# Attention and experts on one core: modality ids in runs, constants on GpSimd, first k load from ScalarE, another order table

## The chip, the core and the metric

One core of a Trainium2 chip runs the whole kernel. The metric is the time of one execution on the device in microseconds (us). Engines are named as in the profile: PE (TensorE matmul; PEld is its weight load), DVE (VectorE), ACT (ScalarE), POOL (GpSimd), SP (SyncE, which here mostly issues DMAs). An engine works through its own instructions strictly in the order in which they were written, so an instruction that waits holds up all that stand behind it on that engine.

## The reference, cut to what matters

Two stages. First attention with a compressive memory for B=4, H=8, S=576, D=64; its output, as a matrix x of 2304 tokens by 512, then goes through a mixture of 8 experts, of which each token uses one.

```python
scores = scale * q @ k.T                       # causal, 576x576 per head
a = softmax(scores);  local = a @ v
q_p = elu(q) + 1
mem_out = (q_p @ M_prev) / (q_p @ z_prev + 1e-6)
x = g * mem_out + (1 - g) * local              # g = sigmoid(beta), per head

logits = x @ w_gate + modality_bias[modality_id]
e = argmax(logits);  gate_w = softmax(logits)[e]
out = gate_w * (relu(x @ w1[e]) @ w2[e])       # 512 -> 1024 -> 512 per token
```

`modality_id` holds one 64 bit integer (0 or 1) per token. It is needed only as a bias of the gate's logits.

## The kernel before

**Attention** runs over 16 pairs of heads (4 batches of 4 pairs). For each pair: `load_t` fetches q, k and v (two DMAs for q, two for k, three for v, issued by SP into two buffers each, `qn`, `kn`, `vn`); `prep` turns q and k on PE (L617), copies them out of PSUM (`qT`, `kT`, `move`, L605 on ACT or L607 on DVE by the table `ENG`), takes exp(q) on ACT (L630) and makes `ph` from it in three POOL steps (L633, L635, L637); `scores` does q·k on PE (L652), a row minimum with the mask on DVE (L665) and the exp on ACT (L671); `ptrans` turns the probabilities on PE (L688) and copies them to `pt`; `av` multiplies with v (L708); `memory` does the memory read (L739) and `combine` puts both together into `xb` (DVE L777, POOL L782). Once a batch is done, `gate` stores `xb` to `x_dram` (L789), turns it (L801), computes logits (L814) and copies them to `lgs` (L820). `route` makes the expert index of each token and its place in the expert's list, and scatters token numbers into three tables in DRAM, `tbl` (L887); `rank` then counts how many tokens the largest expert has so far (L903, L904).

**Experts.** After the first batch the expert with most tokens is known (`perm0`, L902); `load_w` brings its weights in 16 pieces of 128x512 (L945) through three staging buffers (`xg` twice, `osb`), and splits each into a high part made by ACT (L952) and a low part made by DVE or POOL in turn (L956). `slot` then multiplies 256 gathered tokens: turn (L1009), first matrix (L1031), second (L1053), always as three products of high and low parts. The first slots of the largest expert are mixed into attention's last batches, so that PE has work while it waits there; the rest (another expert's weights, its slots, small remainders) comes when attention is over. A loop at the end does tiles that were left over; here it has none.

**Setup.** `setup` fills constants. POOL writes the mask, zero pads and index rows. DVE makes seven small constants in `small2` (L484 to L490). POOL's `table` (L495) fills a block with a sentinel; it lies in the first part of `xb`, and SP writes it from there into the three tables (L504), plus one zero row (L505). `consts` (L507) loads the gate's weights, the biases and the modality ids: five DMAs put each id into its own partition, 8 bytes each (L513, L515). POOL turns them into a bias per token (`consts2`, L525 to L529).

**The order** of all this is written down by a planner, `Plan`: every step carries an engine, an estimated duration, what it reads and writes, and a priority. The priority is a place in the program plus a number from the table `EARLIER` (stage, part of the program, engine). The planner walks in estimated time and takes for each engine, out of the steps that could start within `WINDOW` of the first one, the one of lowest priority. `ENG` says for each kind of copy, and each quarter of attention, whether ACT or DVE does it. The numbers in both tables were found by a search. While PE has nothing else in the beginning, 90 small matmuls on ones (`warm`, L563) are put into its gaps.

Of the kernel before, what the change touches and what calls it, by code (L numbers as in the profile page):

```python
# [226 lines left out]
def kernel(  # L227
# [89 lines left out]
    EARLIER = {
        "av": ((37990, 64809, -34114, 0, 0), (17172, -53738, 532, 0, 0),
               (-47025, -61069, -2874, 0, 0), (6424, 17552, -8223, 0, 0)),
        "bet": ((0, -613, 17881, 0, -169047), (0, 0, 0, 0, 0), (0, 0, 0, 0, 0), (0, 0, 0, 0, 0)),  # L320
        "c": ((1994, 0, 12754, -23788, 0), (349, 0, 2076, -62209, 0),
              (3614, 0, -9647, -56606, 0), (44924, 0, 7322, -42973, 0)),
        "con": ((0, 0, -18237, -36160, -17681), (0, 0, 0, 0, 0), (0, 0, 0, 0, 0), (0, 0, 0, 0, 0)),
# [1059 lines left out]
```

## Time and profile before

| | |
|---|---|
| median of 3 runs | 457.66 us (457.32 to 458.00) |
| the profiled execution | 458.25 us, of which the profile's span is 456.5 us |
| PE busy | 432.2 us, 95% of the span, 4230 instructions |
| DVE, ACT, POOL busy | 241.5, 234.3, 202.4 us (53, 51, 44%) |
| mean granted clock of PE | 0.976 |
| DMA | 42.96 MB, 82092 packets, 70848 of them under 512 B |

The shares are means over two very different halves. In the first, attention loads PE, DVE and ACT all near the full; in the second PE multiplies experts and the others have little to do. A busy PE is not a PE at its peak, since matmuls are pipelined and their ends are modelled. So the table says little of what a change is worth: that is read from stretches of the time line and from what ended each wait.

### The profile page before, as it was taken

The numbers are of one execution on the slowest core, as the hardware profiler recorded it, in microseconds if no ns is written. First come the engines' busy times: TensorE is split into PE (matmuls) and PEld (weight loads), VectorE is DVE, ScalarE is ACT, GpSimd is POOL, SyncE is SP. The second block draws the span as 40 slices with busy tenths as digits, with TensorE's granted clock in tenths as the row PEclk, the third lists the DMA queues.
The fourth block names the chain that finished last, engine by engine and source line by source line (L and its number), as shares of the span: only waits on it lengthen the run. The fifth ranks groups of instructions, "written<-read, shape, count | busy, mean of one in ns | idle before, by whom it ended". The sixth has DMA issues, their size and how long they took to land. (4 is left out here: it accounts for less than half of the span.)

```text
span 456.5 us, 11508 instructions
## 1 busy us (share of the span) xinstructions
PE 432.2 (95%) x4230; PEld 349.8 (77%) x4230; DVE 241.5 (53%) x882; ACT 234.3 (51%) x683; POOL 202.4 (44%) x214
## 2 busy tenths in 40 slices
PE   8998999989979999999999999999999999999991
PEld 6786877657746788776678998988889888898980
DVE  3997997888867967878336964131113013111200
ACT  2897989779977957873234344131123124121310
POOL 8786775768845967554365131303010140001100
PEclk8999999989979999999899999999999999999997
DMA  7666336565569503140027666303000046100100
GB/s 151 139 105 142 81 73 157 152 109 138 135 145 252 127 2 73 31 131 2 2 81 211 105 185 199 103 24 95 6 28 0 24 150 202 66 24 24 47 22 22
DMA packets 82092, 42.96 MB, mean 94 GB/s; under 512 B 70848, under 2 KB 71232, under 8 KB 82034
## 3 DMA queue, kind: packets, MB, share of 16 engines
q1 hardware_dynamic: 78354, 32.55, 29.7%
q0 software_dynamic: 3680, 9.66, 6.5%
q8 instruction: 34, 0.56, 0.6%
q14 instruction: 24, 0.20, 0.1%
HBM read 32.29 MB, written 10.10 MB: 93 GB/s over the span
## 5 line engine op out<-in xcount | busy, mean ns | idle before, releaser
L671 ACT ACTIVATE P<-P,nm 128x448 f32<-128x448 f32 (+4 forms) x160 | 88.4, 558 | 10.7 <-DVE nm L665 10.6
L991 POOL DMA_INDIRECT out_dram<-osb,ids x20 | 19.8, 992 | 153.3 <-ACT osb L1060 82.9
L1031 PE MATMUL pa<-xh,w1h 128*128 128x256 f32 (+2 forms) x288 | 84.1, 292 | 0.9 <-issue 0.8
L1031 PE MATMUL pa<-xl,w1h 128*128 128x256 f32 (+2 forms) x288 | 82.5, 286 | 0.0
L1031 PE MATMUL pa<-xh,w1l 128*128 128x256 f32 (+2 forms) x288 | 82.3, 286 | 0.0
L1042 DVE SCALAR_TENSOR_TENSOR hlo<-pa,hh 128x256 fp32r<-128x256 f32 (+1 forms) x72 | 29.3, 413 | 94.2 <-ACT hh L1040 89.2
L652 PE MATMUL pa<-kT,qT 64*128 64x320 f32 (+4 forms) x384 | 64.9, 424 | 1.8 <-DVE nm L665 0.8
L665 DVE CUSTOM_DVE_ANT_0 P<-pa,maskw 128x320 f32<-128x320 f32 (+3 forms) x160 | 63.1, 425 | 2.7 <-PE pa L652 2.3
L1053 PE MATMUL pa<-w2h,hh 128*128 128x512 f32 (+1 forms) x152 | 60.7, 400 | 0.0
L1053 PE MATMUL pa<-w2l,hh 128*128 128x512 f32 (+1 forms) x152 | 59.9, 394 | 0.0
L1040 ACT ACTIVATE hh<-pa 128x256 fp32r<-128x256 f32 (+1 forms) x80 | 29.0, 367 | 58.8 <-PE pa L1031 45.4
L1031 PEld LDWEIGHTS pa<-xh,w1h 128*128 128x128 f32 x288 | 54.5, 189 | 4.2 <-issue 2.0
L1053 PE MATMUL pa<-w2h,hlo 128*128 128x512 f32 (+1 forms) x144 | 56.9, 395 | 0.0
L1031 PEld LDWEIGHTS pa<-xl,w1h 128*128 128x128 f32 x288 | 54.5, 189 | 1.3 <-issue 0.7
L1031 PEld LDWEIGHTS pa<-xh,w1l 128*128 128x128 f32 x288 | 54.6, 189 | 0.0
L1060 ACT ACTIVATE osb<-pa,ids 128x512 f32<-128x512 f32 (+1 forms) x19 | 13.1, 688 | 74.0 <-PE pa L1053 73.4
L708 PE MATMUL pa<-pt,vn 128*64 128x64 f32 (+4 forms) x384 | 49.3, 407 | 0.2 <-DVE nm L665 0.2
L708 PEld LDWEIGHTS pa<-pt,vn 128*64 128x64 f32 x384 | 24.0, 142 | 29.1 <-issue 21.4
L652 PEld LDWEIGHTS pa<-kT,qT 64*128 64x128 f32 x384 | 40.2, 192 | 7.6 <-DVE nm L665 2.0
L688 PE MATMUL pa<-ident,P 64*128 64x64 f32 x832 | 39.2, 229 | 5.6 <-ACT kT L605 2.7
L688 PEld LDWEIGHTS pa<-ident,P 64*128 64x128 f32 x832 | 35.0, 143 | 10.1 <-issue 2.8
L607 DVE COPY pt<-pa 128x512 f32<-128x512 f32 (+2 forms) x64 | 34.0, 569 | 6.8 <-PE pa L688 6.6
(202 smaller groups left out, 751.5 us busy)
## 6 DMA issues: line engine op xcount, KB each, us to landing
raw<-in_moe_w_dram SPq DMA_DIRECT2D x32, 256.0 KB
vn<-in_v_dram SPq DMA_DIRECT2D x32, 128.0 KB
x_dram<-xb SPq DMA_DIRECT2D x4, 1024.0 KB
xg<-in_moe_w_dram SPq DMA_DIRECT2D x11, 256.0 KB
qn<-in_q_dram SPq DMA_DIRECT2D x16, 160.0 KB
kn<-in_k_dram SPq DMA_DIRECT2D x16, 160.0 KB
qn<-in_q_dram SPq DMA_DIRECT2D x16, 128.0 KB
kn<-in_k_dram SPq DMA_DIRECT2D x16, 128.0 KB
```

The costliest lines, as they stand in the source:

```text
L607: g.op("DVE", dve_ns(n), lambda: nc.vector.tensor_copy(dst(), src()), r=r, w=w, prio=prio)
L652: nc.tensor.matmul(t[hh].ap[:, o:o + z - x], lhsT=q_[HALF[hh], tok0(j):tok0(j) + P], rhs=k_[HALF[hh], x:z], start=True, stop=True)
L665: nc.vector.tensor_tensor_reduce(out=pj[:, x:z], in0=t.ap[0:m, o:o + z - x], in1=mk, scale=-SCALE, scalar=nm if x else 3.0e38, op0=ALU.add ...
L671: g.op("ACT", act_ns(w, False, 2), lambda pj=pj, nm=nm, den=den, w=w: nc.scalar.activation(out=pj[:, 0:w], in_=pj[:, 0:w], func=AF.Exp, sc ...
L688: nc.tensor.transpose(t[u].ap[:, 64 * n:64 * n + 64], prow[c][j][r_, kb * P:(kb + 1) * P], ident[r_, r_])
L708: nc.tensor.matmul(dst.ap[HALF[hh], c0:c0 + n], lhsT=v_[:, kb, hh], rhs=f[hh][:, 64 * u0:64 * u0 + n], start=first, stop=last)
L991: g.op("POOL", 1310, lambda: nc.gpsimd.indirect_dma_start(out=out[:, :], out_offset=bass.IndirectOffsetOnAxis(ap=ids[u % 4][0:m, t, 0:1].b ...
L1031: nc.tensor.matmul(hp.ap[:, 0:n_], lhsT=a[:, c, f * P:(f + 1) * P], rhs=x_[:, c, 0:n_], start=(n == 0), stop=(n == 3 * KC - 1))
L1040: g.op("ACT", act_ns(z - a), lambda f=f, hp=hp, i=i, a=a, z=z: nc.scalar.activation(out=hh[i][:, f, 0:z - a], in_=hp.ap[:, a:z], func=AF.R ...
L1042: g.op("DVE", dve_ns(z - a), lambda f=f, hp=hp, i=i, a=a, z=z: nc.vector.scalar_tensor_tensor(out=hlo[i][:, f, 0:z - a], in0=hp.ap[:, a:z] ...
L1053: nc.tensor.matmul(op.ap[0:m], lhsT=a[:, f, ts], rhs=w_[:, f], start=(y == 0 and n == 0), stop=(y == 3 and n == 5))
L1060: g.op("ACT", act_ns(512, True, 1), lambda t=t, op=op, oi=oi: nc.scalar.activation(out=osb[oi][0:m], in_=op.ap[0:m], func=AF.Copy, scale=i ...
```

## The change

1. The modality ids are loaded as runs: 20 partitions of 128 ids each (the five DMAs become two). POOL casts them, one PE transpose turns them so that each token has its partition, and two ACT copies (`turned`) put them into `modf`. They use the second half of `xg` as scratch.
2. The seven small constants move from DVE (`small2`) to POOL (`consts1`).
3. The sentinel block lies in `lgs` instead of `xb`, and the zero row in `xg`.
4. The first k load is issued by ACT instead of SP.
5. `load_w` can have high halves made by DVE, by the entry `wh` of `ENG`. That entry is (A, A).
6. `rank` loses a multiply and a sum; the count is carried on, with one fused instruction in `route` for the two middle batches, and in the last batch it counts, a multiply and an add become one instruction.
7. The planner's costs of some DMAs are changed, some entries of `ENG` move between ACT and DVE, and all numbers of `EARLIER`, `STICK` and `WINDOW` are new.

```diff
-        "q0": (V, V, V, V), "q1": (V, V, V, V), "k0": (A, A, A, V), "k1": (A, A, A, A), "av0": (V, A, A, V),
-        "av1": (V, A, V, V), "g0": (A, A, A, A), "g1": (V, A, V, V), "m0": (A, A, A, A), "m1": (V, A, A, A),
-        "p00": (V, A, V, A), "p01": (A, V, V, V), "p10": (A, V, A, V), "p11": (V, A, A, A), "wl": (V, G),
+        "q0": (V, V, V, V), "q1": (V, V, V, V), "k0": (V, A, A, V), "k1": (A, A, A, A), "av0": (V, A, V, V),
+        "av1": (V, A, V, V), "g0": (A, V, A, A), "g1": (V, A, V, V), "m0": (V, V, A, A), "m1": (A, A, A, A),
+        "p00": (A, A, V, A), "p01": (A, V, V, V), "p10": (A, V, A, A), "p11": (V, A, A, V), "wh": (A, A),
+        "wl": (V, G),
...
-    Plan.WINDOW = dict(zip(("PE", "ACT", "DVE", "POOL", "SP"), (6, 95, 1, 671, 3308)))
+    Plan.WINDOW = dict(zip(("PE", "ACT", "DVE", "POOL", "SP"), (5, 102, 0, 342, 4832)))
...
-        def small2():
-            v.tensor_copy(iote, iot_i)
-            v.tensor_scalar(out=eoff, in0=iote, scalar1=float(NT), scalar2=None, op0=ALU.mult)
...
-        sent = xb[0].rearrange("p j d -> p (j d)")[:, 0:2 * NROW // P].bitcast(I32)
-        zrow = xb[0][0:1, 1]
+        sent = lgs[:, 0:2 * NROW // P].bitcast(I32)
...
-            nc.sync.dma_start(out=x_dram[NT:NT + 1, :], in_=zrow)
+            nc.sync.dma_start(out=x_dram[NT:NT + 1, :], in_=xg[0][0:1, 0])
...
-            nc.sync.dma_start(out=modi[0:64, :, 0], in_=mod32[:, 0:64].rearrange("b p w -> p b w"))
-            for j in range(1, NB):
-                nc.sync.dma_start(out=modi[:, :, j], in_=mod32[:, QS[j]:QE[j]].rearrange("b p w -> p b w"))
+            nc.sync.dma_start(out=m20[0:B * NB - B], in_=mod32[:, 128:2 * S].rearrange("b (j x) -> b j x", x=2 * P))
+            nc.sync.dma_start(out=m20[B * NB - B:B * NB, 0:P], in_=mod32[:, 0:P])
...
+        def consts1():
+            gp.tensor_copy(iote, iot_i)
+            gp.tensor_scalar(out=eoff, in0=iote, scalar1=float(NT), scalar2=None, op0=ALU.mult)
...
+            gp.tensor_copy(mf20, m20[0:B * NB].rearrange("q (p w) -> q p w", w=2)[:, :, 0])
+
+        def turned():
+            nc.scalar.activation(out=modf[:, :, 1:NB], in_=tm.ap[:, 0:B * NB - B].rearrange("p (b j) -> p b j", b=B), func=AF.Copy)
+            nc.scalar.activation(out=modf[:, :, 0], in_=tm.ap[:, B * NB - B:B * NB], func=AF.Copy)
...
+        g.op("PE", 70, lambda: nc.tensor.transpose(tm.ap[:, 0:B * NB], mf20, ident[0:B * NB, 0:B * NB]),
+             r=[("xg", 0, 1)], w=[tm], alloc=tm, prio=("con", 3))
...
+            on = nc.sync if eng == "SP" else nc.scalar
...
-            g.op("SP", emit=e, w=[(nm, n)], prio=prio, **dma_ns((575, 610), (525, 610), (600, 250)))
+            g.op("SP", emit=e, w=[(nm, n)], prio=prio, **dma_ns((575, 620), (525, 620), (600, 160)))
...
-            g.op("SP", emit=e2, w=[(nm, n)], prio=prio, **dma_ns((575, 600), (600, 550)))
+            g.op(eng, emit=e2, w=[(nm, n)], prio=prio, **dma_ns((575, 750), (600, 600)))
...
+            if 0 < b < B - 1:
+                v.tensor_tensor_reduce(out=rk, in0=s2.ap[:, 0:E], in1=oh0, scale=1.0, scalar=cnt, op0=ALU.mult,
+                                       op1=ALU.add, accum_out=cnt)
...
-            v.tensor_tensor(out=rk, in0=basec, in1=oh0, op=ALU.mult)
-            v.tensor_reduce(out=cnt, in_=rk, axis=AX.X, op=ALU.add)
...
+            if w == 0 and r == 0 and ENG["wh"][i % 2] == V:
+                g.op("DVE", 335, lambda i=i, t=t: nc.vector.tensor_copy(parts(i)[0], raws()[t]), r=[k_], w=[("wh",) + c],
+                     prio=prio, port=True)
...
-        load_t("k", k, p, -9 + p)
+        load_t("k", k, p, -9 + p, "ACT" if p == 0 else "SP")
```

What stands in a row changes at many places. Three of them follow. Line numbers of the changed kernel are other than those of the kernel before: its L580 and L581 are the q and k loads, L585 the v load, L615 and L613 the copies on DVE and ACT, L673 and L679 the minimum and the exp, L965 the high half of a weight piece.

DVE at the start, before: the copies of the second q (qT), the seven constants, then the first row minima (P is the probabilities' buffer, nm the minimum).

```order
L607 COPY qT_144<-pa_95 128x256
L484 CAST iote<-iot_i 128x8
L485 TENSOR_SCALAR eoff<-iote 128x8
L486 TENSOR_SCALAR iot_69<-iote 128x8
L487 MEMSET basec 128x8
L488 MEMSET nst 128x8
L489 COPY i8b<-iot_69 128x40
L490 MEMSET i8b 64x8
L665 ISA P_3_154,nm_171<-pa_96,maskw 128x448
L665 ISA nm_171 128x1
```

DVE at the start, after:

```order
L615 COPY kT_144<-pa_89 128x320
L536 TENSOR_SCALAR gg<-gg 128x16
L537 RECIPROCAL gg<-gg 128x16
L540 COPY gm<-gg 64x4 x2
L615 COPY qT_142<-pa_91 128x320
L615 COPY qT_142<-pa_92 128x256
L615 COPY qT_143<-pa_93 128x320
L615 COPY qT_143<-pa_94 128x256
L673 ISA P_3_153,nm_170<-pa_95,maskw 128x448
L673 ISA nm_170 128x1
```

The seven constants are gone from between the copies and the first minimum, and DVE has got one copy of the first k in front.

SP, before: the constants' loads, the sentinel tables and the loads around them.

```order
L508 DMA wgs<-in_moe_w_gate_dram 128x4x8
L509 DMA bias_72<-in_moe_modality_bias_dram 128x16
L513 DMA modi<-in_moe_modality_id_dram 64x4x2
L515 DMA modi<-in_moe_modality_id_dram 128x4x2 x4
L577 DMA vn_141<-in_v_dram 128x4x64 x2
L578 DMA vn_141<-in_v_dram 64x2x64
L504 DMA tbl_61<-xb_187 128x288
L504 DMA tbl_62<-xb_187 128x288
L504 DMA tbl_63<-xb_187 128x288
L505 DMA x_dram<-xb_187 1x512
```

SP, after, the same place:

```order
L500 DMA wgs<-in_moe_w_gate_dram 128x4x8
L501 DMA bias_72<-in_moe_modality_bias_dram 128x16
L505 DMA xg_106<-in_moe_modality_id_dram 16x1x256
L506 DMA xg_106<-in_moe_modality_id_dram 4x128
L492 DMA tbl_61<-lgs 128x288
L492 DMA tbl_62<-lgs 128x288
L492 DMA tbl_63<-lgs 128x288
L493 DMA x_dram<-xg_106 1x512
L585 DMA vn_140<-in_v_dram 128x4x64 x2
L586 DMA vn_140<-in_v_dram 64x2x64
```

The ids take two DMAs instead of five, the tables are read out of `lgs` instead of `xb`, and they are written before the v load instead of behind it.

ACT among the weight pieces of the first expert, before (w2h is the high half, xg and osb the staging buffers, kT the turned k, pt the turned probabilities):

```order
L952 ACTIVATE w2h_99<-xg_107 128x512
L630 ACTIVATE ex_147<-pa_94 128x256
L605 ACTIVATE pt_176<-pa_90 128x8x64
L605 ACTIVATE pt_176<-pa_95 128x6x64
L952 ACTIVATE w2h_99<-xg_107 128x512
L671 ACTIVATE P_2_153,nden<-P_2_153,nm_171 128x320
L605 ACTIVATE kT_145<-pa_89 128x320
L605 ACTIVATE kT_145<-pa_95 128x256
L952 ACTIVATE w2h_99<-osb_112 128x512
```

ACT, after, the same three pieces and the next:

```order
L965 ACTIVATE w2h_98<-xg_106 128x512
L613 ACTIVATE pt_174<-pa_88 128x8x64
L965 ACTIVATE w2h_98<-xg_106 128x512
L965 ACTIVATE w2h_98<-osb_111 128x512
L613 ACTIVATE pt_175<-pa_94 128x8x64
L613 ACTIVATE pt_175<-pa_91 128x6x64
L679 ACTIVATE P_2_152,nden<-P_2_152,nm_170 128x320
L679 ACTIVATE P_2_157,nden<-P_2_157,nm_171 128x320
L679 ACTIVATE P_4_154,nden<-P_4_154,nm_170 128x576
L679 ACTIVATE P_0_150,nden<-P_0_150,nm_170 64x64
L965 ACTIVATE w2h_98<-xg_106 128x512
```

The three pieces now stand close together and the copies of the next k (kT) come later than all three; on SP their three loads stand in a row, ahead of the pair's q and k loads, where before a q load stood between the first and the second.

## Rows read from the trace of the kernel before

**Rows 1.** Stretches: us; busy us (instructions) per engine; PE's granted clock; DMA share; GB/s.

```profile
60.00:80.00 20.00, 20.00 (x293) 14.17 (x292) 16.73 (x71) 18.40 (x62) 14.09 (x10) 1.00 0.51 125
...
300.00:350.00 50.00, 50.00 (x290) 43.86 (x289) 10.91 (x33) 12.83 (x33) 7.95 (x8) 1.00 0.12 35
```

**Rows 2.** Time line, the start: start us, us, engine line op, [idle before <- what ended it].

```profile
2.69 0.65 SPq L572 DMA_DIRECT2D kn<-in_k_dram  x1
...
3.64 0.31 ACT L549 ACTIVATE gg<-bet 128x8 f32<-128x8 f32 x2 [1.57 <-DMA bet<-in_beta_dram]
...
4.08 0.65 SPq L572 DMA_DIRECT2D qn<-in_q_dram  x1
...
5.33 0.46 PE L617 MATMUL pa<-ident,qn 64*128 64x64 f32 x8 [0.23 <-DMA qn<-in_q_dram]
...
6.92 0.46 PE L617 MATMUL pa<-ident,kn 64*128 64x64 f32 x8 [0.51 <-DMA kn<-in_k_dram]
...
8.34 0.69 PE L617 MATMUL pa<-ident,qn 64*128 64x64 f32 x8 [0.39 <-DMA qn<-in_q_dram]
...
8.82 1.80 PE L652 MATMUL pa<-kT,qT 64*128 64x448 f32 x4
...
9.93 0.88 DVE L484 CAST iote<-iot_i 128x8 f32<-128x8 int32 x1
...
10.43 0.74 PE L617 MATMUL pa<-ident,kn 64*128 64x64 f32 x9
...
11.10 0.93 PE L563 MATMUL pa<-ones 128*128 128x128 bf16 x10
...
11.95 0.81 PE L652 MATMUL pa<-kT,qT 64*128 64x320 f32 x4
...
12.84 0.62 DVE L665 CUSTOM_DVE_ANT_0 P<-pa,maskw 128x448 f32<-128x448 f32 x1
...
13.94 0.48 DVE L665 CUSTOM_DVE_ANT_0 P<-pa,maskw 128x320 f32<-128x320 f32 x1
```

**Rows 3.** Stretch of the first loads, columns as in the first group.

```profile
5.00:10.00 5.00, 3.83 (x38) 2.48 (x39) 1.72 (x5) 1.43 (x4) 4.85 (x27) 0.81 0.96 199
```

**Rows 4.** Time line around the sentinel tables and the ids.

```profile
37.12 1.52 SPq L504 DMA_DIRECT2D tbl<-xb  x3
...
37.27 0.20 POOL L525 CAST modf<-modi 128x20 f32<-128x20 int32 x1 [3.28 <-DMA modi<-in_moe_modality_id_dram]
...
40.40 0.55 DVE L777 SCALAR_TENSOR_TENSOR xb<-pa,gg,rnd 128x320 f32<-128x320 f32 x1 [3.11 <-DMA tbl<-xb]
```

**Rows 5.** Waits of ACT between 30 and 50 us: total us, times, longest.

```profile
ACT P L671 <- DVE nm L665: 2.8, 3, 1.8
```

**Rows 6.** Time line of PE: where `av` of four pairs (the 2nd, 3rd, 8th, 9th) starts.

```profile
36.98 2.92 PE L708 MATMUL pa<-pt,vn 128*64 128x64 f32 x24
...
51.71 2.92 PE L708 MATMUL pa<-pt,vn 128*64 128x64 f32 x24
...
111.98 2.92 PE L708 MATMUL pa<-pt,vn 128*64 128x64 f32 x24
...
122.42 2.92 PE L708 MATMUL pa<-pt,vn 128*64 128x64 f32 x24
```

**Rows 7.** Time line of `rank`'s two instructions and of a small ACT copy.

```profile
88.13 0.21 DVE L903 TENSOR_TENSOR rk<-basec,oh 128x8 f32<-128x8 f32 x1
...
88.67 0.23 ACT L605 ACTIVATE ot<-pa 128x64 f32<-128x64 f32 x1
```

**Rows 8.** Time line of a late weight piece, and who waited for ACT behind it.

```profile
130.86 0.63 ACT L952 ACTIVATE w2h<-xg 128x512 fp32r<-128x512 f32 x1 [2.92 <-DMA xg<-in_moe_w_dram]
...
132.41 0.69 PE L688 MATMUL pa<-ident,P 64*128 64x64 f32 x7 [2.66 <-ACT kT L605]
```

**Rows 9.** The two stretches behind that wait, columns as in the first group.

```profile
130.00:135.00 5.00, 2.59 (x16) 1.30 (x17) 1.67 (x5) 4.14 (x11) 3.05 (x3) 0.60 0.51 106
135.00:140.00 5.00, 5.00 (x47) 2.61 (x48) 2.21 (x9) 2.64 (x11) 0.89 (x1) 0.72 0.59 187
```

More of the change, by code (lines that the diff above doesn't have):

```diff
@@ L313 @@
     NPR = B * NP
-    Plan.STICK = 38058
-    Plan.WINDOW = dict(zip(("PE", "ACT", "DVE", "POOL", "SP"), (6, 95, 1, 671, 3308)))
+    Plan.STICK = 41813
+    Plan.WINDOW = dict(zip(("PE", "ACT", "DVE", "POOL", "SP"), (5, 102, 0, 342, 4832)))
     EARLIER = {
[L318 to L323, printed above, removed]
[50 rows of a table removed]
-        "tab": ((0, 0, 0, 0, 15191), (0, 0, 0, 0, 0), (0, 0, 0, 0, 0), (0, 0, 0, 0, 0)),
[3 rows of a table removed]
-        "warm": ((0, 0, 0, 0, 0), (71039, 0, 0, 0, 0), (0, 0, 0, 0, 0), (0, 0, 0, 0, 0)),
+        "av": ((-38083, 143719, -19216, 0, 0), (30814, -48506, -58022, 0, 0),
+               (-75111, -79059, 16304, 0, 0), (41629, -35195, -19098, 0, 0)),
+        "bet": ((0, 9095, 6730, 0, -181455), (0, 0, 0, 0, 0), (0, 0, 0, 0, 0), (0, 0, 0, 0, 0)),
+        "c": ((3549, 0, 70652, -82457, 0), (-338, 0, -32458, -66686, 0),
+              (2399, 0, -49174, -97336, 0), (48019, 0, 74728, -37405, 0)),
+        "con": ((26991, -46264, 0, 33823, 4165), (0, 0, 0, 0, 0), (0, 0, 0, 0, 0), (0, 0, 0, 0, 0)),
[50 rows of a table added]
+        "tab": ((0, 0, 0, 0, 9077), (0, 0, 0, 0, 0), (0, 0, 0, 0, 0), (0, 0, 0, 0, 0)),
[3 rows of a table added]
+        "warm": ((0, 0, 0, 0, 0), (108849, 0, 0, 0, 0), (0, 0, 0, 0, 0), (0, 0, 0, 0, 0)),
     }
@@ L542, in setup @@
              prio=-9)
-        g.op("POOL", 2900, small, r=["ones"], w=["iot", "tri", "pr", "rex", "modi", "thr", "wg", ("mt", 0), ("mt", 1)] +
+        g.op("POOL", 2900, small, r=["ones"], w=["iot", "tri", "pr", "rex", "thr", "wg", ("mt", 0), ("mt", 1)] +
              [("nd", i, h, j) for i in range(4) for h in range(2) for j in range(NB)], prio=-8)
-        g.op("DVE", 1100, small2, r=["iot"], w=["iote", "basec", "nst"], prio=("con", 3))
         g.op("SP", emit=lambda: nc.sync.dma_start(out=bet, in_=beta.unsqueeze(0).to_broadcast([P, H])), w=["bet"],
@@ L551, in setup @@
         g.op("DVE", 900, gates, w=["gg", "gm"], prio=("bet", -3))
-        g.op("POOL", 1660, table, w=[("xb", i) for i in range(NP)] + [("xg", 0, 0), ("xg", 0, 1)], prio=-3)
-        g.op("SP", emit=table2, r=[("xb", i) for i in range(NP)], w=[("tbl", j) for j in range(NTB)], prio=("tab", 4),
+        g.op("POOL", 1660, table, w=["lgs", ("xg", 0, 0), ("xg", 0, 1)], prio=-3)
+        g.op("SP", emit=table2, r=["lgs", ("xg", 0, 0)], w=[("tbl", j) for j in range(NTB)], prio=("tab", 4),
              **dma_ns(*[(450, 410)] * 3, (450, 6)))
-        g.op("SP", emit=consts, w=["wg", "modi"], prio=("con", 3),
-             **dma_ns((540, 224), (540, 56), (625, 30), *[(550, 60)] * 4, lat=1500))
-        g.op("POOL", 1900, consts2, r=["modi"], w=["lb", "lgs"], prio=("con", 3))
+        g.op("SP", emit=consts, r=["iot"], w=["wg", ("xg", 0, 1)], prio=("con", 3),
+             **dma_ns((540, 224), (540, 56), (450, 60), (450, 30), lat=1300))
+        g.op("POOL", 1450, consts1, r=["iot"], w=[("xg", 0, 1), "iote", "basec", "nst"], prio=("con", 3))
+        g.op("PE", 70, lambda: nc.tensor.transpose(tm.ap[:, 0:B * NB], mf20, ident[0:B * NB, 0:B * NB]),
+             r=[("xg", 0, 1)], w=[tm], alloc=tm, prio=("con", 3))
+        g.op("ACT", 160, turned, r=[tm], w=["modf"], prio=("con", 3))
+        g.op("POOL", 1700, consts2, r=["modf", "wg"], w=["lb", ("xg", 0, 1)], prio=("con", 3))
     def warm():
@@ L908, in e @@
             if b == B - 2:
-                v.tensor_scalar(out=rk, in0=oh0, scalar1=-2.0 * NT, scalar2=None, op0=ALU.mult)
-                v.tensor_tensor(out=rk, in0=rk, in1=basec, op=ALU.add)
+                v.scalar_tensor_tensor(out=rk, in0=oh0, scalar=-2.0 * NT, in1=basec, op0=ALU.mult, op1=ALU.add)
                 v.max(out=top, in_=rk)
                 v.max_index(out=perm1, in_max=top, in_values=rk)
-        g.op("DVE", 1000, e, r=["basec"], w=["nst"] + ([("perm", 0)] if b == 0 else []) +
+        g.op("DVE", 1000 if b % 2 == 0 else 500, e, r=["basec", "cnt"], w=["nst", "cnt"] + ([("perm", 0)] if b == 0 else []) +
              ([("perm", 1)] if b == B - 2 else []), prio=prio)
@@ L951, in load_w @@
             g.op("SP", emit=lambda i=i, t=t: load(i, t), r=avail, w=[k_], prio=prio, **dma_ns((450, 728)))
-            g.op("ACT", act_ns(512, False), lambda i=i, t=t: nc.scalar.activation(
-                out=parts(i)[0], in_=raws()[t], func=AF.Copy), r=[k_], w=[("wh",) + c], prio=prio)
+            if w == 0 and r == 0 and ENG["wh"][i % 2] == V:
+                g.op("DVE", 335, lambda i=i, t=t: nc.vector.tensor_copy(parts(i)[0], raws()[t]), r=[k_], w=[("wh",) + c],
+                     prio=prio, port=True)
+            else:
+                g.op("ACT", act_ns(512, False), lambda i=i, t=t: nc.scalar.activation(
+                    out=parts(i)[0], in_=raws()[t], func=AF.Copy), r=[k_], w=[("wh",) + c], prio=prio)
             lo = ENG["wl"][i % 2] if w == 0 and r == 0 else "DVE"
```

30 lines of the change are left out of this document (15 added, 15 removed), and 106 rows, old and new, of the table EARLIER.

## The prediction, written before the result was known

> **What bounds the kernel now.** I read the stretches first, for where each engine is full; then the waits of PE, ACT and DVE; then the time line at the places where one of them stands still. In the second half PE alone is full and ACT and DVE are a quarter busy [rows 1]: there a change on another engine gives nothing. In the first half PE, DVE and ACT are all nearly full: in 60 to 80 us PE 20.0 of 20, ACT 18.4, DVE 16.7 [rows 1]. The best measure of attention's pace is the distance between the `av` steps of neighbouring pairs: 122.42 - 111.98 = 10.4 us where nothing is in the way, but 51.71 - 36.98 = 14.7 us in another place [rows 6]. So a pair needs about 10.4 us and the holes come on top. Holes in the first half count in full, if they are in the chain, because the order of PE's expert work behind the last routing is the same in both kernels: what comes earlier there ends earlier. Three holes can be seen.
>
> The first is the start. The first row minimum on DVE begins at 12.84, though its matmuls began at 8.82; from 9.93 on DVE makes the seven constants, 12.84 - 9.93 = 2.9 us [rows 2]. The second is at 37 us: DVE waits 3.1 us with its write of `xb` until the DMA of the sentinel tables, issued at 37.12, has read that same buffer [rows 4]; ACT loses 2.8 us behind it [rows 5]. The third is a weight piece that came late: ACT waits 2.9 us for its DMA, the copy of k behind it on ACT is late, PE waits 2.7 us for that, and the granted clock of the next two stretches is 0.60 and 0.72 [rows 8, 9], a mixture of its two levels of 1.2 and 2.4 GHz after PE had stood idle.
>
> **The change part by part.** *Constants off DVE.* Removed: 2.9 us ahead of the first minimum [rows 2]. What is late next: two minima of 0.6 us can run at once (their matmuls are at 8.82 to 10.62), and the third needs the matmuls at 11.95, which wait for the second k (turned at 10.43) and stand behind ten warm matmuls of 0.93 us [rows 2], of which the new order leaves two. So the third minimum comes at about 11.95 - 0.93 x 8/10 + 0.8 = 12.0 instead of 13.94: 1.9 us earlier. The gain lies between 0, if ACT's exps or later loads pace the start, and 2.9 us; I take **-2.0** for the start, since DVE and ACT are nearly full from there on and keep what they get. On POOL the same seven instructions, and the cast of the ids, take the place of its wait of 3.3 us for the ids [rows 4]; at 0.2 us for each (its small cast there took 0.20) they are 1.6 us, so POOL is not later: 0. If that cover were gone they would cost POOL 1.6 us.
>
> *First k load on ACT.* It takes the issue of one load, 4.08 - 2.69 = 1.4 us, out of SP's row, so that the second q and k are issued that much earlier. But PE could turn the four loads only 1.6, 1.4 and 2.1 us apart (5.33, 6.92, 8.34, 10.43, the first three held by the DMA [rows 2]), and the DMA engines' share was 0.96 from 5 to 10 us [rows 3]: the transfers themselves were the limit. Bounds 0 and -1.4; I take **-0.3**, near the end of a full DMA. ACT waits until 3.64 for `bet` anyway [rows 2], so its two issues (1.4 us by SP's) and its table load behind them are hidden; uncovered they would cost that 1.4 us. Moving the first v load ahead of the third pair's q and k can make those land later, by one load's 1.4 to 2.1 us [rows 2]; they are turned only behind the second pair's first minima, so I take 0, at worst that +2.1. The Trainium skill has a rule that speaks against this part: in "DMA: Bandwidth & Descriptors", section "Issuing engines are not separate DMA queues", DMAs from SP, ACT and POOL run on the same 16 DMA engines, and issuing from several saves only the sequencer's time. The 0.96 here agrees. By that rule the term is near 0; if the issue were all that counted, the sum would be 1.1 us lower.
>
> *Sentinel in another buffer.* Nothing that DVE does at 37 us waits for the tables any more; `lgs` is first written at the first gate, `xg` by the first weights, both tens of us later. DVE's wait is 3.1 us [rows 4], ACT's loss behind it 2.8 [rows 5], and the pace there is 14.7 against 10.4 us [rows 6], 4.3 us of which this hole is one part. Next in line is PE's own 10.4 us. Bounds 0 (if ACT alone paces) and -3.1; I take **-2.5**, a little under ACT's loss.
>
> *Ids in runs.* POOL's wait of 3.3 us [rows 4] becomes shorter; POOL is not on the chain there, so 0. Added: one PE transpose of 20 rows, hidden or below 0.3 us, and two ACT copies at 0.23 us [rows 7] on a full engine: **+0.4** with their waits. Bounds 0 and +0.7; more only if PE, which stands in order, reaches the transpose before the ids have come, which the order places behind the second `av`: that was at 37 us [rows 6], and the ids came at 37.3 [rows 4].
>
> *`rank`.* Two DVE instructions of some 0.2 us [rows 7] fall away three times and one comes back twice: **-0.2**, bounds -1.2 and +0.2. The weights' loads do not wait for them. *High halves on DVE.* The entry is (A, A), so nothing is moved: 0.
>
> *The order.* The third hole is worth up to 2.7 us of idle PE and, by the clock, 5 x 0.40 + 5 x 0.28 = 3.4 us: 6.1 us [rows 8, 9]. In the new order the three loads follow each other ahead of the pair's q and k, and the copy of k stands behind the three pieces instead of between them, so I give it an even chance to go: -3.0. Any new order can make such a hole elsewhere; at one in three of the same price it costs 2.0. Together **-1.0**, bounds -6.1 and +6.1.
>
> **The sum.** -2.0 - 0.3 - 2.5 + 0.4 - 0.2 - 1.0 = -5.6 us. The profiled execution took 458.25 us, of which 456.5 is the span; its sum is 452.65. The median of the runs is 0.6 us under that execution, so I forecast **452.1 us**.
>
> **The rivals.** *Absorbed.* PE or ACT set the pace of the first half by themselves, and DVE's holes were cover: for it speaks that ACT is at 18.4 of 20 us [rows 1], against it that ACT itself lost 2.8 us behind DVE [rows 5]. Then of the start and the table's hole a third remains, -1.5, and the rest gives -0.5: 457.7 - 2.0 = 455.7. *Both ways lucky.* The third hole goes and no other comes: 457.7 - 4.6 - 6.1 = 447. *A new late piece, slower.* In the new order the last weight piece is issued behind the second batch's store to `x_dram`, and ACT reaches it a few instructions on. If its DMA lands after that, ACT waits, PE waits for the copies behind it, and the clock falls: 6.1 us at the price of [rows 8, 9]. It decides from a wait of some 2.5 us on, with the old hole still there: 457.7 - 4.6 + 6.1 = 459.2, slower. For it speaks that the plan which let the first such wait happen was made in the same way; against it that the planner's costs of q and k loads were raised. *It doesn't do what it says.* No high half is made on DVE, and the first k load may bring nothing by the rule above; neither changes the sum by more than 0.3. *Nothing left.* All is absorbed and the new order is as good as the old: 457.7.
>
> **How the numbers follow.** Forecast, 449 to 454.9: 0.53. Absorbed, about 455.7: 0.17. Lucky, about 447: 0.08. Nothing left: 0.09. A new late piece, 459.2: 0.13. A measurement of this kernel can tell about 0.2% from no change, 0.9 us. Faster by more: 0.53 + 0.17 + 0.08 = 0.78; within: 0.09; slower: 0.13. The range leaves out the lucky case's lower half and most of the slower one: 448 to 458.5.
>
> **What would show it.** Right: the first minimum on DVE near 10 us and the third near 12; no wait of DVE for the `tbl` DMA, and some 11 to 12 us between the second and third `av`; no wait of ACT of over 1 us for a weight piece and no stretch under 0.8 of the clock between 125 and 145 us; attention's last routing 5 to 6 us earlier and all behind it as long as before. Wrong: an `av` distance over 14 us in a new place, PE waiting for the transposed ids, or ACT waiting for the last weight piece. If the last routing comes earlier but the end does not, my reading of the second half is wrong.

## The result, and the profile after

The changed kernel takes 453.19 us in the median (451.18 to 454.18, four runs) against 457.49 us for the kernel before on the same chip: ratio 0.9899, 95% interval 0.9863 to 0.9935, 4.3 us less. The profiled execution of after took 453.65 us with a span of 451.9, against 458.25 and 456.5 before, so its trace has 4.6 us to account for. The forecast was 452.1 us. The time agrees; two of the terms behind it do not.

The engines are as full as before. The first line of the page of after (engine, busy us, share of the span, instructions):

```profile
PE 428.7 (95%) x4231; PEld 351.3 (78%) x4231; DVE 238.7 (53%) x882; ACT 235.0 (52%) x676; POOL 203.1 (45%) x219
```

The start, which was to give 2.3 us, gave nothing in this trace. Time line of after, to be read against [rows 2] (start, duration, engine, line, operation, idle time before and what ended it):

```profile
6.36 0.46 PE L625 MATMUL pa<-ident,kn 64*128 64x64 f32 x8 [1.31 <-DMA kn<-in_k_dram]
...
7.13 0.52 PE L625 MATMUL pa<-ident,qn 64*128 64x64 f32 x9
...
10.75 0.74 PE L625 MATMUL pa<-ident,kn 64*128 64x64 f32 x9
...
11.12 0.62 DVE L673 CUSTOM_DVE_ANT_0 P<-pa,maskw 128x448 f32<-128x448 f32 x1 [1.04 <-PE pa L660]
...
11.75 3.63 PE L660 MATMUL pa<-kT,qT 64*128 64x320 f32 x14
...
13.21 0.49 DVE L673 CUSTOM_DVE_ANT_0 P<-pa,maskw 128x320 f32<-128x320 f32 x1 [0.52 <-PE pa L660]
```

The first pair's k and q are both turned at 7.13 (6.92 before), the second pair's at 10.75 (10.43 before): neither pair is earlier. DVE, now without the constants, waits 1.04 us for PE at 11.12, and the third minimum is at 13.21 instead of 13.94. The first `av` comes 1.15 us later than before (29.44 against 28.29, the first line below).

The second hole is gone. PE's first `av` step in before, then the first three in after:

```profile
28.29 2.93 PE L708 MATMUL pa<-pt,vn 128*64 128x64 f32 x24
```

```profile
29.44 0.77 PE L716 MATMUL pa<-pt,vn 128*64 128x64 f32 x6
...
39.57 0.77 PE L716 MATMUL pa<-pt,vn 128*64 128x64 f32 x6
...
49.05 1.20 PE L716 MATMUL pa<-pt,vn 128*64 128x64 f32 x8
```

First to third: 19.6 us, where before needed 51.71 - 28.29 = 23.4 (the third is in [rows 6]). The order of the steps between them differs, so the first-to-third distance is the fair one. DVE's longest wait from 30 to 50 us is 1.0 us, for PE; the wait for the table [rows 4] is not there. GpSimd's wait for the ids [rows 4] is gone as well: the cast of the ids waits for nothing, and the wait for the turned ids stands behind the sum into `xb`, which begins at 41.34:

```profile
35.76 0.28 POOL L529 CAST xg<-xg 20x128 f32<-20x128 int32 x1
...
45.94 0.46 POOL L516 TENSOR_TENSOR lb<-modf,bias 128x160 f32<-128x160 f32 x1 [1.78 <-ACT modf L533]
```

The third hole [rows 8, 9] shrank. Stretches of after (window; length, PE, PEld, DVE, ACT and POOL busy; granted clock; DMA share; GB/s), and ACT's longest wait for a weight piece:

```profile
10.00:15.00 5.00, 5.00 (x29) 3.66 (x27) 2.57 (x10) 3.00 (x9) 4.92 (x6) 0.51 1.21 191
...
130.00:135.00 5.00, 5.00 (x97) 3.95 (x92) 4.91 (x13) 5.00 (x15) 2.84 (x3) 1.00 0.83 263
135.00:140.00 5.00, 3.91 (x53) 2.62 (x51) 4.86 (x19) 4.33 (x14) 4.03 (x4) 1.00 1.13 254
...
205.00:210.00 5.00, 3.35 (x42) 3.35 (x44) 3.32 (x16) 3.74 (x11) 1.78 (x2) 0.61 0.07 6
210.00:215.00 5.00, 5.00 (x37) 3.33 (x35) 1.78 (x7) 0.57 (x2) 2.39 (x2) 0.71 0.00 0
```

```profile
126.04 0.63 ACT L965 ACTIVATE w2h<-osb 128x512 fp32r<-128x512 f32 x1 [1.44 <-DMA osb<-in_moe_w_dram]
```

In 130 to 140 us the clock is 1.00 (0.60 and 0.72 before) and ACT waits 1.44 us instead of 2.92. But there are two new places: the clock of 0.51 in 10 to 15 us (0.85 before), and 0.61 and 0.71 behind a standstill that before does not have:

```profile
205.82 0.49 DVE L673 CUSTOM_DVE_ANT_0 P<-pa,maskw 128x320 f32<-128x320 f32 x1 [3.81 <-remote]
206.07 0.60 ACT L613 ACTIVATE pt<-pa 128x512 f32<-128x512 f32 x1 [3.86 <-remote]
...
206.65 0.69 PE L696 MATMUL pa<-ident,P 64*128 64x64 f32 x7 [2.42 <-DVE nm L673]
```

DVE and ACT stood still for 3.8 us with a releaser that the profile gives only as "remote", and PE then waited 2.42 us for DVE.

The last routing begins with PE's turn of the logits, in before and in after:

```profile
241.60 0.58 PE L832 MATMUL pa<-ident,lgs 128*128 128x128 f32 x3
```

```profile
236.08 0.58 PE L840 MATMUL pa<-ident,lgs 128*128 128x128 f32 x3
```

The balance of the two traces: start +1.15 us up to the first `av`; first to third `av` -3.8; third `av` to the last routing 189.9 to 187.0, -2.9; from there to the end 214.9 to 215.8, +0.9. Together -4.6.

### The profile page after: what moved, and what is told of

Its sections match the earlier page's. It is cut to its first block, busy times and chain, and to the rows that moved or that the text cites. A ratio compares the mean times of both kernels' runs of the same rounds, so it can differ in the third digit from the quotient of the medians.

```text
span 451.9 us, 11518 instructions
## 1 busy us (share of the span) xinstructions
PE 428.7 (95%) x4231; PEld 351.3 (78%) x4231; DVE 238.7 (53%) x882; ACT 235.0 (52%) x676; POOL 203.1 (45%) x219
## 5 line engine op out<-in xcount | busy, mean ns | idle before, releaser
L679 ACT ACTIVATE P<-P,nm 128x192 f32<-128x192 f32 (+4 forms) x160 | 88.5, 560 | 10.6 <-DVE nm L673 7.7
L1004 POOL DMA_INDIRECT out_dram<-osb,ids x20 | 19.6, 982 | 154.3 <-ACT osb L1073 86.6
L673 DVE CUSTOM_DVE_ANT_0 P<-pa,maskw 128x320 f32<-128x320 f32 (+3 forms) x160 | 62.5, 428 | 9.4 <-remote 3.8
L716 PE MATMUL pa<-pt,vn 128*64 128x64 f32 (+4 forms) x384 | 47.3, 393 | 2.4 <-DMA vn<-in_v_dram 1.2
L716 PEld LDWEIGHTS pa<-pt,vn 128*64 128x64 f32 x384 | 24.2, 137 | 27.0 <-issue 17.5
L696 PE MATMUL pa<-ident,P 64*128 64x64 f32 x832 | 40.3, 229 | 4.8 <-DVE nm L673 4.4
L613 ACT ACTIVATE pt<-pa 128x512 f32<-128x512 f32 (+2 forms) x74 | 37.6, 548 | 13.2 <-PE pa L716 4.9
```

What stands on the lines that cost most here:

```text
L613: g.op("ACT", act_ns(n), lambda: nc.scalar.activation(out=dst(), in_=src(), func=AF.Copy), r=r, w=w, prio=prio)
L673: nc.vector.tensor_tensor_reduce(out=pj[:, x:z], in0=t.ap[0:m, o:o + z - x], in1=mk, scale=-SCALE, scalar=nm if x else 3.0e38, op0=ALU.add ...
L679: g.op("ACT", act_ns(w, False, 2), lambda pj=pj, nm=nm, den=den, w=w: nc.scalar.activation(out=pj[:, 0:w], in_=pj[:, 0:w], func=AF.Exp, sc ...
L696: nc.tensor.transpose(t[u].ap[:, 64 * n:64 * n + 64], prow[c][j][r_, kb * P:(kb + 1) * P], ident[r_, r_])
L716: nc.tensor.matmul(dst.ap[HALF[hh], c0:c0 + n], lhsT=v_[:, kb, hh], rhs=f[hh][:, 64 * u0:64 * u0 + n], start=first, stop=last)
L1004: g.op("POOL", 1310, lambda: nc.gpsimd.indirect_dma_start(out=out[:, :], out_offset=bass.IndirectOffsetOnAxis(ap=ids[u % 4][0:m, t, 0:1].b ...
```

## Experiments

Twelve kernels ran, in three sets of four. In all but the third and the fourth run the order of before or of after was written out instruction for instruction, so nothing moves but the edit (line numbers are about ten higher). Chips differ: before took 455.6, 448.1 and 455.4 us beside the three sets, so times are compared only as ratios to before. The ratio is not the quotient of the two medians: that is 0.992 for e5 and 0.996 for e1 and e11. The sizes in us, each from one trace, and PE's granted clock from 10 to 15 us (e1 and e2 are from one chip, e5 from another, e9 to e12 from a third; beside after, before took 457.5 us):

| kernel | order | clock | third minimum | first `av` | 1st to 3rd `av` | 3rd `av` to last routing | ratio to before (95%) |
|---|---|---|---|---|---|---|---|
| before | before | 0.85 | 13.94 | 28.29 | 23.4 | 189.9 | |
| e9 before again | before | 0.75 | 13.90 | 28.26 | 25.1 | 186.9 | 0.9996 (0.9963 to 1.0029) |
| e1 table | before | 1.00 | 12.51 | 26.86 | 24.2 | 188.4 | 0.9939 (0.9903 to 0.9974) |
| e2 constants | before | 0.73 | 13.41 | 27.78 | 25.4 | 189.6 | 1.0017 (0.9984 to 1.0049) |
| e10 GpSimd's wait | before | 1.00 | 13.98 | 28.34 | 22.8 | 190.4 | 1.0014 (0.9976 to 1.0053) |
| e11 table and wait | before | 0.58 | 13.92 | 28.47 | 20.5 | 189.3 | 0.9960 (0.9932 to 0.9989) |
| e12 the same, constants | before | 1.00 | 12.18 | 26.54 | 20.5 | 186.9 | 0.9979 (0.9950 to 1.0009) |
| after | after | 0.51 | 13.21 | 29.44 | 19.6 | 187.0 | 0.9899 (0.9863 to 0.9935) |
| e5 after again | after | 1.00 | 12.52 | 27.82 | 19.6 | 179.7 | 0.9905 (0.9872 to 0.9938) |

**e1, the table alone.**

```diff
-sent = xb[0].rearrange("p j d -> p (j d)")[:, 0:2 * NROW // P].bitcast(I32)
-zrow = xb[0][0:1, 1]
+sent = lgs[:, 0:2 * NROW // P].bitcast(I32)
+zrow = xg[0][0:1, 0]
...
-gp.memset(zrow, 0.0)
...
```

`consts2`'s scratch moves from `lgs` to `xg` with it, and GpSimd has one memset less at the start.

> The kernel before, every engine's instructions in before's order, with one edit: the sentinel block lies in lgs instead of xb, and the zero row is taken from xg. Theory (the table's hole carries the gain; in the changed kernel the distance from the second to the third av fell from 14.7 to 9.5 us, and by the end 4.6 us were gained): DVE no longer waits 3.1 us at 40 us, the third av comes some 2.5 us earlier and the end 2 to 3 us earlier, 454.5 to 455.5 us against 457.5. Rival (the hole was cover; ACT and PE set the pace): the wait goes, but a wait on PE or ACT takes its place and the end moves by under 1 us, 456.5 or more.

Measured: ratio 0.9939, some 2.8 us less (1.9 us by the medians, 453.74 against 455.64). But not as the theory has it: DVE's wait for the table is gone, and `av` needs 24.2 us from first to third. Time line of e1:

```profile
35.55 2.22 PE L717 MATMUL pa<-pt,vn 128*64 128x64 f32 x14
...
36.34 0.20 POOL L534 CAST modf<-modi 128x20 f32<-128x20 int32 x1 [3.86 <-DMA modi<-in_moe_modality_id_dram]
...
41.33 1.43 POOL L791 TENSOR_TENSOR xb<-xb,mt 128x640 f32<-128x640 f32 x1
...
42.80 0.45 ACT L614 ACTIVATE mt<-pa 128x325 f32<-128x325 f32 x1 [3.44 <-POOL xb L791]
42.80 0.50 DVE L616 COPY mt<-pa 128x325 f32<-128x325 f32 x1 [3.08 <-POOL xb L791]
...
51.02 1.95 PE L717 MATMUL pa<-pt,vn 128*64 128x64 f32 x12
```

GpSimd waits 3.86 us for the ids; its sum into `xb` therefore comes at 41.33, and ACT and DVE, which want to overwrite the `mt` that it reads, wait 3.44 and 3.08 us. The new wait has the size of the old one. In this trace e1 is ahead at the start, by a side effect (last section) and with a full clock: its first `av` comes at 26.86. But the traced execution, 455.57 us, is the longest of its eight, so where the median's gain lies is not shown.

**e2, the constants alone.**

```diff
-v.tensor_copy(iote, iot_i)
...
-v.memset(i8b[64:P, 0], 99.0)
+gp.tensor_copy(iote, iot_i)
...
+gp.memset(i8b[64:P, 0], 99.0)
```

> The kernel before, in before's order, with one edit: the seven small constants are made on GpSimd, just ahead of consts2, instead of on DVE. The forecast's theory: the first row minimum comes at about 10 us instead of 12.84, the third at 12 instead of 13.94, and the end is 2.0 us earlier, 455.5 against 457.5 us. Rival, from the trace of the changed kernel (first minimum 11.12, third 13.21, loads no earlier): DVE then waits for PE or ACT, the third minimum gains under 1 us, and the end is within 1 us of before, 456.5 to 457.5.

Measured: ratio 1.0017, with all seven on GpSimd. The first minimum is at 10.37 as forecast, the third at 13.41, the end not earlier; a gain of 2 us lies outside the interval (at most 0.7). The traced execution, 460.23 us, is the second longest of twelve. In it the first `av` is 0.5 us earlier than in before, and the hole takes that back: DVE waits at its write of `xb` until 40.16, for the zero row's DMA, the last behind the tables', and in before until 40.40 [rows 4]; GpSimd's sum into `xb` then begins at 42.21 and 42.26. The tables' DMAs were issued at 36.98 there, at 37.12 in before.

```profile
40.16 0.55 DVE L787 SCALAR_TENSOR_TENSOR xb<-pa,gg,rnd 128x320 f32<-128x320 f32 x1 [3.38 <-DMA x_dram<-xb]
```

**e3, the code without its numbers, and e4, the numbers without the code.** Here the planner lays the order anew.

```diff
e3, after:   ENG, EARLIER, STICK, WINDOW, dma_ns   -> those of before
e4, before:  ENG, EARLIER, STICK, WINDOW, dma_ns   -> those of after
```

> The changed kernel's code in all its parts (constants on GpSimd, ids in runs, sentinel in lgs, first k load issued by ScalarE, v0's load cost, rank), but with the numbers of before: the engine table, due times, windows and DMA costs, so that the order is planned from these. Theory (the code carries the gain, the searched numbers little): the table's hole is gone and the end is some 3 us earlier than before, 454 to 455 us. Rival (the numbers carry it, the third hole above all, or the numbers only fit the old code): no gain, 457 to 460 us, with a wait of ACT for a weight piece of over 2 us between 100 and 145 us still there.

> The code of before with the changed kernel's numbers: engine table, due times, windows and DMA costs; the order is planned from these. Theory (the code carries the gain): DVE still waits some 3 us for the table's DMA near 40 us, the late weight piece may be gone, 456 to 458 us. Rival (the numbers carry it): 453 to 454.5 us, as the changed kernel, with the last routing 5 us earlier than before's 241.6.

Measured: e3 1.0023 (0.9995 to 1.0052), no gain; e4 1.0149 (1.0104 to 1.0194), slower. Of the expectations on a gain from one half, neither came true. e3's time is as its rival has it, but without that rival's wait of over 2 us for a weight piece (the longest was 1.10). Time line of e3:

```profile
33.85 1.39 PE L715 MATMUL pa<-pt,vn 128*64 128x64 f32 x6 [0.61 <-ACT kT L612]
...
37.51 2.22 DVE L614 COPY pt<-pa 128x512 f32<-128x512 f32 x4 [5.00 <-PE pa L715]
...
42.10 0.77 PE L715 MATMUL pa<-pt,vn 128*64 128x64 f32 x6
...
53.89 1.57 PE L715 MATMUL pa<-pt,vn 128*64 128x64 f32 x10
```

First to third `av` is 20.0 us, so the hole is closed as in after, but with the old numbers the first `av` comes at 33.85, 5.6 us later than before, and DVE stands still for 5.00 us. In e4 the hole is worse:

```profile
43.63 1.01 DVE L778 SCALAR_TENSOR_TENSOR xb<-pa,gg,rnd 128x320 f32<-128x320 f32 x2 [4.37 <-DMA tbl<-xb]
```

**e5, the changed kernel again.** No edit; the order is written out.

> The changed kernel again, its order unchanged instruction for instruction, for the other three to stand against. In the changed kernel's profile DVE and ACT stood still for 3.8 us at 202 to 206 us and the granted clock fell to 0.61 and 0.71 behind it. Theory (this belongs to the order, a wait that the trace does not name): the hole is there again, at the same place, and the time is 453 us. Rival (it came in that execution alone): it is not there, the profiled execution is 2 to 4 us shorter than 453.65, and the times of the runs spread over some 3 us.

Measured: ratio 0.9905, so the gain is there on another chip as well. The standstill near 200 us came once more, at 2.43 us:

```profile
199.04 0.49 DVE L683 CUSTOM_DVE_ANT_0 P<-pa,maskw 128x320 f32<-128x320 f32 x1 [2.43 <-remote]
```

It is in both traces of exactly this order (3.81 in after, 2.43 here) and in none of e6 to e8, which differ from it by one step at the start. So the theory held as far as this repeat goes, at a smaller size; whether the wait belongs to the order or to the execution is open, and so is what "remote" stands for.

**e6, the first k load issued by SP again.**

```diff
-load_t("k", k, p, -9 + p, "ACT" if p == 0 else "SP")
+load_t("k", k, p, -9 + p)
```

> The changed kernel with the first k load issued by SP again, ahead of the first q, all else in the same order. Theory (the four loads at the start are bound by their transfer, not by their issue): the first four loads are turned within 0.5 us of the changed kernel's times, and the end is the same within 0.5 us, 453.2. Rival (issue counts): every load behind it comes 1.4 us later and the end is 1 to 1.4 us later, 454.5.

On SP the load stands ahead of the first q. Measured: ratio 0.9894, the same as e5. Time line of e6:

```profile
5.25 0.69 PE L635 MATMUL pa<-ident,kn 64*128 64x64 f32 x8 [0.24 <-DMA kn<-in_k_dram]
...
7.10 0.69 PE L635 MATMUL pa<-ident,qn 64*128 64x64 f32 x8 [0.22 <-DMA qn<-in_q_dram]
...
10.74 0.74 PE L635 MATMUL pa<-ident,kn 64*128 64x64 f32 x9
```

The first k is turned 1.15 us earlier than in e5 (6.40), the last of the four at 10.74 against 10.65. The first half of the theory was too narrow, the second held: with a second issuing engine the first k was turned later and the last load at the same time. I take it that k and q then share the transfer. The Trainium skill has in "DMA: Bandwidth & Descriptors", section "Issuing engines are not separate DMA queues", that DMAs of several engines interleave on the same 16 DMA engines and that issuing from several saves only the sequencer's time. The last load's 10.74 against 10.65 agrees.

**e7, the first v load behind the third pair's q and k.**

```diff
 SP  q1, k1
-SP  v0
 SP  q2, k2
+SP  v0
```

> The changed kernel with the first v load issued behind the third pair's q and k loads, where before had it, all else in the same order. Theory (v's transfer lies in the way of q and k at the start; k1 was turned at 10.75, against 10.43 before, though its issue was earlier): the second k is turned 0.5 to 1.5 us earlier, the first av comes earlier and the end by some 0.5 to 1 us, 452.5. Rival (the transfer hides under the second pair's scores): the end is the same, 453.2, or later if the first av then waits for v.

Measured: ratio 0.9915 (0.9872 to 0.9958), the same. The second k was turned at 10.99, not earlier than e5's 10.65: so v's transfer is not seen in its way. The theory fell.

**e8, more warm matmuls.**

```diff
+for _ in range(1 + {29: 32, 39: 7, 40: 9}.get(i, 0)):
     nc.tensor.matmul(t.ap[:, 0:P], lhsT=ones, rhs=ones, start=True, stop=True)
```

> The changed kernel with 48 more warm matmuls on PE in its idle times ahead of the second to fourth turn at the start, and the one that stood behind the fourth moved ahead of it, all else in the same order. In the changed kernel the granted clock was 0.51 from 10 to 15 us (0.85 before), and sixteen score matmuls there took 4.01 us. Theory (the half clock at the start costs what the constants' removal gave): the granted clock of 10 to 15 us is above 0.8, the third row minimum comes near 12 us instead of 13.21, the end is 1 to 2 us earlier, 451.5. Rival (loads and ACT pace the start whatever the clock): the clock rises and the end stays, 453.2; or the extra matmuls stand in the way and it is later.

Measured: ratio 0.9882 (0.9836 to 0.9928), not to be told from e5. The granted clock from 10 to 15 us was 1.00, but in e5, e6 and e7 it was 1.00 there too, without the extra matmuls: the 0.51 of after was that execution's. So the experiment had nothing to repair and doesn't test its theory. What the half clock goes with can be read from after and e5, which have one order, though they are not from one set of runs: the third minimum at 13.21 against 12.52 and the first `av` at 29.44 against 27.82.

**e9 to e12, the two waits one by one.** In e10 `consts2` on GpSimd stands behind the next `xb` sum; e11 adds e1's edit, e12 e2's.

```diff
-POOL  consts2
 POOL  mt, xb sum, ph, ph of the next pair
+POOL  consts2
```

> The kernel before again, its order unchanged instruction for instruction, for the other three to stand against, with a trace of its own from the same chip. Theory (holes that belong to the order come in every execution; what differs belongs to the execution): DVE waits some 3 us for the table's DMA near 40 us and the distance of the second to the third av is 14 to 15 us again; ACT's wait for the weight piece near 130 us (2.9 us in the first trace, 2.1 and 2.0 us in the table and constants runs) lies anywhere from 1 to 3 us. Rival: all waits are the same within 0.3 us. The seven constants on DVE took 2.9 us in the first trace and 1.6 us in the table run, where GpSimd began its work 0.5 us earlier: 2.9 us again if GpSimd's place decides, 1.6 us if the execution does.

> The kernel before, in before's order, with one edit: consts2 (the cast of the ids and four small instructions on GpSimd) stands behind the next xb sum instead of ahead of it, so that GpSimd waits for the ids in front of nothing that is needed. Theory (two waits guard one place: in the table run the table's wait was gone, but GpSimd's wait of 3.9 us for the ids let ACT and DVE wait 3.4 and 3.1 us for xb, and the distance of the second to the third av was 15.5 us): with the ids' wait alone taken away the table's 3.1 us stay, the distance stays 14 to 15.5 us, and the end is within 1 us of before. Rival (GpSimd's wait alone is the hole): distance 11 to 12 us and the end some 3 us earlier.

> Both together in before's order: the sentinel block in lgs, and consts2 on GpSimd behind the next xb sum. Theory (two waits guard one place; only both together open it): no wait of DVE for the table, no wait of ACT or DVE of over 1 us for GpSimd's xb near 42 us, distance of the second to the third av 11.5 to 12.5 us, the third av 3 us earlier than in the run of before, and the end 2.5 to 3.5 us earlier. Rival (a third wait stands behind the two, or the time is given back later): distance 14 us or more, or the end under 1.5 us earlier.

> As the run with both, and the seven small constants made on GpSimd where consts2 stood. Theory (the start is paced by the loads; the constants gave nothing when moved alone, ratio 1.002): the same as the run with both within 1 us, and GpSimd's 1.6 us more are hidden. Rival of the forecast (the constants are 2 us on the path, and only the table's hole hid them): 2 us less than the run with both.

Measured: e9 is before again, ratio 0.9996. Its two holes stand where they stood; second to third `av` is 16.4 us, more than expected, with a clock of 0.50 from 45 to 50 us:

```profile
40.74 0.55 DVE L787 SCALAR_TENSOR_TENSOR xb<-pa,gg,rnd 128x320 f32<-128x320 f32 x1 [3.48 <-DMA tbl<-xb]
...
130.89 0.63 ACT L962 ACTIVATE w2h<-xg 128x512 fp32r<-128x512 f32 x1 [2.57 <-DMA xg<-in_moe_w_dram]
```

e10, GpSimd's wait alone taken away: 1.0014, no gain, 22.8 us from first to third `av`.

```profile
37.03 0.77 PE L718 MATMUL pa<-pt,vn 128*64 128x64 f32 x6
...
39.85 0.55 DVE L787 SCALAR_TENSOR_TENSOR xb<-pa,gg,rnd 128x320 f32<-128x320 f32 x1 [2.51 <-PE pa L718]
...
51.16 1.57 PE L718 MATMUL pa<-pt,vn 128*64 128x64 f32 x10
```

DVE still waits 2.51 us at the same instruction. The profile names PE's `av` there, which this instruction doesn't read; the table's DMAs had been issued from 36.51 on, so I take it for the table's wait. No row shows the landing, but in e11, which differs from e10 in the table's place alone, the same instruction begins at 37.40 without a wait. e11, both taken away:

```profile
37.16 0.77 PE L717 MATMUL pa<-pt,vn 128*64 128x64 f32 x6
...
37.40 0.54 DVE L786 SCALAR_TENSOR_TENSOR xb<-pa,gg,rnd 128x320 f32<-128x320 f32 x1
...
41.45 0.45 ACT L614 ACTIVATE mt<-pa 128x325 f32<-128x325 f32 x1 [0.48 <-PE pa L748]
...
48.94 1.57 PE L717 MATMUL pa<-pt,vn 128*64 128x64 f32 x10
```

The `mt` copy on ACT waits 0.48 us and second to third `av` is 11.8 us, against 14.7 in before and 16.4 in e9; first to third is 20.5 against 23.4 and 25.1. (e9's clock was 0.50 from 45 to 50 us; in before, e10 and e11 it was 1.00 there.) So two waits guarded one place, and only both edits open it: shown in the traces, one of each kernel. The times do not show it: e11 gains 0.40% by its ratio (0.11 to 0.68), 1.8 us, less than the 2.5 to 3.5 expected, and not to be told from e1's 0.61% with the first edit alone. From third `av` to last routing e11 needs 189.3 us and e9 186.9: part is given back there, in these executions behind a weight piece that ACT waited 1.71 us for at 139.

e12 has the start just as forecast, minima at 9.94 and 12.18, and in that one execution the last routing is 4.3 us earlier than in e11 (233.91 against 238.24).

```profile
12.18 0.49 DVE L674 CUSTOM_DVE_ANT_0 P<-pa,maskw 128x320 f32<-128x320 f32 x1 [1.06 <-PE pa L661]
...
26.54 1.20 PE L717 MATMUL pa<-pt,vn 128*64 128x64 f32 x8
```

But it is the shortest of the twelve executions (451.40 of 451.40 to 455.98 us), and their ratio is not better than e11's (0.9979 against 0.9960). Nor could it be by much: in e11 the constants on DVE take only 1.4 us (last section), and at a clock of 1.00 a start with them so short (e1, first `av` at 26.86) is 0.3 us behind e12's. That is less than the intervals can tell.

## Why the prediction was right, and where it was not

**The sum** was -5.6, the traces give -4.6 and the medians -4.3. It came out near because errors cancelled: the start, forecast at -2.3, came out at +1.15 (in e5, the same order at a full clock, its first `av` is 0.5 us ahead of before's), and the hole and the order gave more than I took. That is luck. The prediction took 0.2% as what a measurement can tell; the intervals here are 0.3 to 0.45% to either side.

**Constants off DVE (forecast -2.0): the lead is there, the way from it to the end failed.** With a full clock the third minimum comes at 12.18 (e12), as worked out, against 13.98 in e10 with the constants on DVE. In before's order this lead reaches the first `av` whole, since that stands 14.4 us behind the third minimum in six of the seven traces (14.55 in e11): 26.54 against 28.34. The failed step is that DVE and ACT "keep what they get". Three things took from it. The table's wait ends by the DMA's time and swallowed e2's 0.5 us. After's order needs 15.3 us from the third minimum to the first `av` in e5 to e8, so its first `av` at a clock of 1.00 is at 27.82 and not at 26.5. And the clock of 0.51 in after's own trace goes with another 1.6 us (29.44). How much of the lead is left at the end is not shown: e2 gains nothing that its runs can show, and e12 against e11 compares too little.

**First k load on ACT (-0.3) and v's place (0): right**, as far as runs can tell: e6 and e7 change nothing, with intervals of 0.4% to either side.

**Sentinel in another buffer (-2.5) and ids in runs (+0.4): right together, wrong apart.** The failed step is "POOL is not on the chain there, so 0", and with it "next in line is PE's own 10.4 us". Next in line was GpSimd's wait for the ids, as long as the table's (e1). I had read in [rows 4] that GpSimd waits 3.28 us for the ids at 37.27, three microseconds ahead of DVE's wait, but did not ask who waits for what GpSimd does next. The change takes away both, so the place gave 3.8 us in its trace instead of 2.1. In before's order the two edits give 2.9 us in the trace (23.4 to 20.5) and 1.8 us in the time. e10 and e11 move `consts2`; no run has the ids in runs alone, so what that part does by itself is not shown.

**The order (-1.0): the size was too small, the mechanism half right.** The traces give -2.9 to the last routing, in spite of the 3.8 us standstill at 202 to 206, and +0.9 behind it. (From the last routing to the end it is 213.3 to 215.7 us in the seven traces of before's order and 215.8 to 218.6 in five of after's, so part of what the order gains is given back there.) The late weight piece is not cured: in seven traces of before's order ACT's longest such wait is 1.7 to 2.9 us, in five of after's order it is 0.5, 1.4, 1.4, 2.0 and 2.5. But it costs less there: a stretch with the clock under 0.95 from 120 to 150 us is in six of those seven traces and in one of these five. Four of the five are from the chip on which before took 448.1 us, where before's order was not traced, so the chip may have its part in that. In ratios, after has 0.9899 and 0.9905 where the two waits alone give 0.9960; the other 0.55 to 0.6%, some 0.4% by e5's medians, is what the new order and the small parts bring together, compared across sets of runs. e3 and e4 show that neither code nor numbers bring it alone. Which shift in the order does, I did not isolate.

**What would show it:** the first minimum came at 11.12, not near 10, and the third at 13.21, not 12: wrong. No wait for the table, and no clock under 0.8 from 125 to 145: right. No wait of ACT over 1 us: wrong, it was 1.44. Second to third `av` 11 to 12 us: it was 9.5, with the first to second longer. Last routing 5 to 6 us earlier: right, 5.5. All behind it as long as before: it was 0.9 us longer.

## What to carry to other kernels

Before costing the removal of a wait, follow the next instruction of each engine at that place: a second wait of the same length may guard it, and then removing either one may give nothing there. Follow a lead won at the start up to the next wait that ends at a time of its own, such as a DMA's landing: the lead goes no further than that, as in e2's trace. Compare starts at equal clocks. And a searched order belongs to its code: the numbers on the old code cost 1.5%, the new code under the old numbers gained nothing.
